# Windowed attention into a rational FFN: the order of the work made by a list scheduler in the source

## The chip, the cores and the metric

The kernel runs on one core of a Trainium2 chip. The metric is the device time of one execution in microseconds (us). The engines are PE (TensorE, matmuls), DVE (VectorE), ACT (ScalarE), POOL (GpSimd) and SP (SyncE, which here only issues DMAs). Each engine works through its own instruction queue in order; an instruction at the head that waits for a semaphore holds everything behind it on the same engine.

## The reference

```python
# q, k, v: (8 batches, 8 heads, 576 positions, 64)
scores = q @ k.T / 8                       # masked to 0 <= i - j < 64
x = softmax(scores) @ v                    # -> x: 4608 tokens x 512
h = x @ w_in                               # w_in 512 x 2048
P = a0 + a1*h + a2*h^2 + a3*h^3
Q = 1 + |b0|*|h| + |b1|*h^2
out = (P / (Q + 1e-6)) @ w_out             # w_out 2048 x 512
```

## The kernel before

The 4608 tokens are nine chunks of 512 (`CH`). A chunk's attention is four units (`unit_load`, `unit_scores`, `unit_transpose`, `unit_av`, one for each pair of heads). A unit loads q, k and v on SP, makes scores on PE (L221), takes the maximum and the exponentials (L228 to L242: eight exponentials on ACT, each followed by the read of its sum), normalises (L246), transposes on PE (L253), copies the result to SBUF on ACT (L255), multiplies with v on PE (L264) and splits the result into a high and a low part, `xh` and `xl` (L269, L270). The band mask is added in one of two ways: for the chunks in `PEM` (here 1 and 2) by two more matmuls on PE (L214), for the others by two DVE passes out of PSUM (L232). Normalising is on DVE for chunk 0 and on POOL for the rest.

The FFN of a chunk is sixteen steps, one for each 128 columns of `w_in`; `steps` lists the 144 of them. `ffn1` makes h with twelve matmuls (L279) and then evaluates the rational function, here called the gate: ACT L286, L287, L288, then DVE L289 and L290 (which read h out of PSUM) beside POOL L291, then ACT L294 and L295, then DVE L296 to L299, which leave the quotient as `gh` and `gl`. `ffn2`, issued `LAG` = 2 steps later, is twelve matmuls (L319) into the chunk's output banks. The gate's temporaries (`ah`, `u`, `num`) have two sets, `gh`/`gl` have three, h has two PSUM banks, which the attention's `ps_x` shares; the scores and the transposed tile share one pair of banks.

The weights arrive as int64 views of pairs and are decoded tile by tile (`decode`): a load on SP, ACT L135, POOL L138, DVE L139 and L140, ACT L143, DVE L144. All 32 decodes must be done once, in the first two chunks; those run as half chunks, `phases` = (0, first half), (1, first half), (1, second half), (0, second half). The second half's weight tiles take the SBUF of the pools `ekv` and `eatt`, which serve chunks 0 and 1 and are closed at step 7 (`SWITCH`).

The order in which things are issued comes from `todo`, a table from step to calls (L341 to L374), and from the loop at L390. That order gives the priorities; the framework's own scheduler (`schedule_with_timeline_sim`, L431) then arranges each engine's queue.

Of the kernel before, what the change touches and what calls it, by code (L numbers as in the profile page):

```python
# [9 lines left out]
F32 = mybir.dt.float32  # L10
# [6 lines left out]
WIN = 64  # L17
# [4 lines left out]
SWITCH = 7  # L22
LAG = 2
W_AT = 0, 1, 2, 3
WLEAD = len(W_AT)
NEG = -1.0e30
PEM = 1, 2
QADD = 1.0 + 1e-6


@with_exitstack
def swa_rational_ffn(ctx: ExitStack, tc: tile.TileContext, qT, kT, v, w_in, w_out, a, b, out):
# [88 lines left out]
    def decode(src, hi, lo):

        w = stage.tile([P, 512, 2], U32, name="w_st", bufs=3)
        if len(src.shape) == 3:
            nc.sync.dma_start(out=w.rearrange("p (c n) two -> p c (n two)", c=src.shape[1]), in_=src)
        else:
            nc.sync.dma_start(out=w.rearrange("p n two -> p (n two)"), in_=src)
        low, high = w[:, :, 0], w[:, :, 1]
        c = stage.tile([P, 512], U32, name="w_c")
        cf = c.bitcast(F32)  # L130

        highf = w.bitcast(F32)[:, :, 1]
        nc.scalar.activation(cf, highf, AF.Copy, scale=2.0 ** -111)  # L135


        nc.gpsimd.tensor_scalar(out=highf, in0=highf, scalar1=0.0, scalar2=None, op0=ALU.mult)  # L138
        nc.vector.scalar_tensor_tensor(out=c, in0=c, scalar=3, in1=high, op0=ALU.logical_shift_left, op1=ALU.bitwise_or)  # L139
        nc.vector.scalar_tensor_tensor(out=c, in0=low, scalar=29, in1=c, op0=ALU.logical_shift_right, op1=ALU.bitwise_or)  # L140
        if len(hi.shape) == 3:
            cf = cf.rearrange("p (c n) -> p c n", c=hi.shape[1])
        nc.scalar.activation(hi, cf, AF.Copy, scale=2.0 ** -8)  # L143
        nc.vector.scalar_tensor_tensor(out=lo, in0=cf, scalar=2.0 ** -8, in1=hi.bitcast(F32), op0=ALU.mult, op1=ALU.subtract)  # L144

    def load_w_in(i):
        decode(w_in[i], wi_h[i], wi_l[i])

    def load_w_out(i):
        decode(w_out_v[:, i, :], wo_h[i], wo_l[i])  # L150
# [12 lines left out]
    def unit_load(c, hp):  # L163
        if c < 2:
            q = ekv.tile([P, TC, WIN], F32, name="q")
            kt = ekv.tile([P, TC + 1, WIN], F32, name="kt")
# [28 lines left out]

    def scores_bank(c, hp):
        if c:
            return ps_a.tile([P, 2, 512], F32, name="ps_s")
        return ps_o.tile([P, 2, DO], F32, name="ps_s", tag=f"o{hp % 2}")

    def unit_scores(c, hp):
        u = live[c, hp]
# [4 lines left out]
        on_pe = c in PEM
        if m0 is None:
            mm = mask[:, 1:2, :].broadcast_to([P, PR, P])
        else:  # L210
# [4 lines left out]
        for p in range(PR):
            for z in range(2):
                for e in range(2):
                    j = 2 * p + e
                    k = u["kt"][z * 64:z * 64 + 64].rearrange("p t s -> p (t s)")
                    w = u["kw"][j] * WIN  # L220
                    nc.tensor.matmul(ps[e * 64:e * 64 + 64, z, p * P:(p + 1) * P], u["q"][z * 64:z * 64 + 64, j, :],  # L221
                                     k[:, w:w + P], start=not on_pe, stop=not on_pe or p == PR - 1)
        sm = pool.tile([P, 2 * PR, P], F32, name="sm")
        NR = 2 * PR
        nmx = pool.tile([P, NR], F32, name="nmx")
        if on_pe:
            pss = ps[:, :, 0:PR * P].rearrange("p z (r c) -> p z r c", c=P)
            nc.vector.tensor_reduce(out=nmx.rearrange("p (z r) -> p z r", z=2), in_=pss, axis=AX.X, op=ALU.max, negate=True)  # L228
            nc.vector.scalar_tensor_tensor(out=nmx, in0=nmx, scalar=SCALE, in1=zero, op0=ALU.mult, op1=ALU.add)
        else:  # L230
            for z in range(2):
                nc.vector.scalar_tensor_tensor(out=sm[:, z * PR:(z + 1) * PR, :],  # L232
                                               in0=ps[:, z, 0:PR * P].rearrange("p (r c) -> p r c", c=P), scalar=SCALE,
                                               in1=mm.bitcast(F32), op0=ALU.mult, op1=ALU.add)
            nc.vector.tensor_reduce(out=nmx, in_=sm, axis=AX.X, op=ALU.max, negate=True)
        sums = pool.tile([P, NR], F32, name="sums")
        for j in range(NR):
            if on_pe:
                nc.scalar.activation(sm[:, j, :], ps[:, j // PR, (j % PR) * P:(j % PR + 1) * P], AF.Exp, scale=SCALE,
                                     bias=nmx[:, j:j + 1], accum_out=sums[:, j:j + 1])  # L240
            else:
                nc.scalar.activation(sm[:, j, :], sm[:, j, :], AF.Exp, bias=nmx[:, j:j + 1], accum_out=sums[:, j:j + 1])  # L242
        rs = pool.tile([P, NR], F32, name="rs")
        nc.vector.scalar_tensor_tensor(out=sums, in0=sums, scalar=1e-9, in1=zero, op0=ALU.add, op1=ALU.add)
        nc.vector.reciprocal(out=rs, in_=sums)
        (nc.vector if c < 1 else nc.gpsimd).tensor_tensor(out=sm, in0=sm, in1=rs.unsqueeze(2).broadcast_to([P, NR, P]), op=ALU.mult)  # L246
        u["sm"] = sm

    def unit_transpose(c, hp):
        u = live[c, hp]  # L250
        ps = ps_a.tile([P, 2, 512], F32, name="ps_s")
        for j in range(2 * PR):
            nc.tensor.transpose(ps[:, j // PR, (j % PR) * P:(j % PR + 1) * P], u["sm"][:, j, :], ident)  # L253
        pT = (eatt if c < 2 else att).tile([P, 2, PR * P], F32, name="pT")
        nc.scalar.copy(out=pT, in_=ps[:, :, 0:PR * P])  # L255
        u["pT"] = pT

    def unit_av(c, hp):
        u = live.pop((c, hp))

        ps = ps_h.tile([P, TC, WIN], F32, name="ps_x", tag="h")
        for j in range(TC):
            for z in range(2):
                nc.tensor.matmul(ps[z * 64:z * 64 + 64, j, :], u["vt"][:, u["vw"][j], z * 64:z * 64 + 64],  # L264
                                 u["pT"][:, z, j * WIN:(j + 1) * WIN], start=True, stop=True)
        xh[c, hp] = xp.tile([P, CH], F32R, name=f"xh{hp}")
        xl[c, hp] = xp.tile([P, CH], F32R, name=f"xl{hp}")
        x = ps.rearrange("p t s -> p (t s)")
        nc.scalar.copy(out=xh[c, hp], in_=x)  # L269
# [38 lines left out]
    def ffn2(s):  # L308
# [11 lines left out]
        if not last:  # L320
            return
# [115 lines left out]
```

## Time and profile before

| | us |
|---|---|
| three runs | 1121.77, 1122.4, 1123.28; median 1122.4 |
| profiled execution | 1124.48, its span 1122.7 |
| PE busy in the span | 991.2 |
| DVE, ACT, POOL busy | 797.6, 675.1, 325.8 |
| first FFN matmul | 46.67 |
| FFN matmuls of step 8, 24, 32, 128 begin | 130.3, 249.0, 321.7, 1021.4 |

The last two rows come from the L279 matmuls in order of time, twelve to a step. Between 321.7 and 1021.4 lie six whole chunks with the attention of the next ones woven in; after 1021.4 one chunk is left, without attention. Busy time counts an instruction from its start to its modelled end; matmuls overlap, so a busy PE is not a PE at its peak. PEclk is the clock granted to PE, as a share of full speed.

### The profile page before, as it was taken

How to read it: one execution, taken by the hardware profiler on the slowest of the kernel's cores; microseconds unless marked ns; L12 is line 12 of the kernel's file. 1: busy time of each engine (PE TensorE's matmuls, PEld its weight loads, DVE VectorE, ACT ScalarE, POOL GpSimd, SP SyncE). 2: the span in 40 equal slices, each digit the busy share in tenths (PEclk: the TensorE clock that was granted, in tenths of full speed). 3: DMA queues.
4: the chain of work that ended last, by engine and by line, in shares of the span. 5: the costliest groups of instructions: out<-in, count | busy, mean ns of one | idle time of the engine just before them, and what ended most of it. 6: DMA issues, size and time to landing. Idle time of an engine off the chain costs nothing.

```text
span 1122.7 us, 16288 instructions
## 1 busy us (share of the span) xinstructions
PE 991.2 (88%) x6064; PEld 765.3 (68%) x6064; DVE 797.6 (71%) x1180; ACT 675.1 (60%) x1471; POOL 325.8 (29%) x223
## 2 busy tenths in 40 slices
PE   4657998698888999999989998999899998989997
PEld 3545776576666777677767776777677766778886
DVE  6886779876755777666667676667766666668775
ACT  4765666557654666655656556655665555666654
POOL 3452335532222222222222222222222222222221
PEclk9767999999999999999999999999999999999999
DMA  9621042322213000310031002110121012001001
GB/s 302 228 89 36 1 129 83 106 70 99 61 50 106 18 21 21 107 37 21 20 107 38 20 20 91 39 41 22 57 81 39 20 40 67 1 1 39 1 1 38
DMA packets 38959, 66.47 MB, mean 59 GB/s; under 512 B 5600, under 2 KB 21984, under 8 KB 38880
## 3 DMA queue, kind: packets, MB, share of 16 engines
q1 hardware_dynamic: 38880, 65.43, 18.4%
q8 instruction: 48, 0.79, 0.3%
q14 instruction: 31, 0.25, 0.1%
HBM read 54.92 MB, written 10.49 MB: 58 GB/s over the span
## 4 chain that ended last, share of the span: by engine, by line
PE 31%; ACT 19%; DVE 14%; POOL 12%; issue 10%; DMA 2%; SPq 0%; POOLq 0%; DVEq 0%; ACTq 0%
PE h L279 16%; PE o L319 11%; POOL u L291 7%; ACT sm L242 5%; POOL sm L246 4%; DVE num L298 3%; ACT ah L294 3%; ACT ah L295 3%; PE ps_x L264 3%; DVE num L289 3%; ACT num L287 2%; DVE gh L296 2%; ACT pT L255 2%; DVE u L297 2%; ACT ah L286 2%
## 5 line engine op out<-in xcount | busy, mean ns | idle before, releaser
L291 POOL TENSOR_TENSOR u<-u,ah 128x512 f32<-128x512 f32 x144 | 197.3, 1371 | 541.5 <-DVE num L289 303.6
L319 PE MATMUL o<-wo_h,gl 128*128 128x512 f32 x576 | 240.9, 418 | 50.1 <-DVE gl L299 46.2
L279 PE MATMUL h<-xl,wi_h 128*128 128x512 f32 x576 | 236.6, 411 | 1.4 <-DVE num L290 1.4
L319 PE MATMUL o<-wo_l,gh 128*128 128x512 f32 x576 | 231.9, 403 | 0.0
L319 PE MATMUL o<-wo_h,gh 128*128 128x512 f32 x576 | 231.7, 402 | 0.0
L279 PE MATMUL h<-xh,wi_l 128*128 128x512 f32 x576 | 227.1, 394 | 0.0
L279 PE MATMUL h<-xh,wi_h 128*128 128x512 f32 x576 | 227.1, 394 | 0.0
L296 DVE SCALAR_TENSOR_TENSOR gh<-num,a_sb,ah 128x512 fp32r<-128x512 f32 x144 | 110.1, 765 | 149.1 <-ACT ah L295 148.8
L294 ACT ACTIVATE ah<-u 128x512 f32<-128x512 f32 x144 | 91.0, 632 | 188.6 <-POOL u L291 188.6
L319 PEld LDWEIGHTS o<-wo_h,gl 128*128 128x128 f32 x576 | 111.2, 193 | 101.1 <-DVE gl L299 61.8
L289 DVE TENSOR_TENSOR num<-num,h 128x512 f32<-128x512 f32 x144 | 98.4, 683 | 96.2 <-ACT num L287 96.0
L286 ACT ACTIVATE ah<-h 128x512 f32<-128x512 f32 x144 | 85.5, 593 | 130.7 <-PE h L279 101.3
L279 PEld LDWEIGHTS h<-xl,wi_h 128*128 128x128 f32 x576 | 108.7, 189 | 35.1 <-issue 9.3
L319 PEld LDWEIGHTS o<-wo_h,gh 128*128 128x128 f32 x576 | 111.7, 194 | 26.2
L319 PEld LDWEIGHTS o<-wo_l,gh 128*128 128x128 f32 x576 | 111.8, 194 | 22.2
L279 PEld LDWEIGHTS h<-xh,wi_l 128*128 128x128 f32 x576 | 108.6, 189 | 25.3
L298 DVE SCALAR_TENSOR_TENSOR num<-num,a_sb,u 128x512 f32<-128x512 f32 x144 | 124.0, 861 | 1.7
L279 PEld LDWEIGHTS h<-xh,wi_h 128*128 128x128 f32 x576 | 109.0, 189 | 21.8
L288 ACT ACTIVATE u<-ah,b_sb 128x512 f32<-128x512 f32 x144 | 117.3, 814 | 0.0
L246 POOL TENSOR_TENSOR sm<-sm,rs 128x1024 f32<-128x1024 f32 x32 | 65.2, 2036 | 176.2 <-ACT num L287 83.5
L287 ACT ACTIVATE num<-h,a_sb 128x512 f32<-128x512 f32 x144 | 111.5, 774 | 0.0
L290 DVE SCALAR_TENSOR_TENSOR num<-num,a_sb,h 128x512 f32<-128x512 f32 x144 | 107.1, 744 | 3.1
(51 smaller groups left out, 1119.6 us busy)
## 6 DMA issues: line engine op xcount, KB each, us to landing
out<-ob SPq DMA_DIRECT2D x36, 256.0 KB, 2.0
w_st<-w_in SPq DMA_DIRECT2D x16, 512.0 KB, 4.7
w_st<-w_out SPq DMA_DIRECT2D x16, 512.0 KB, 3.6
vt<-v SPq DMA_DIRECT2D x8, 448.0 KB, 4.9
vt<-v SPq DMA_DIRECT2D x8, 384.0 KB, 4.1
vt<-v SPq DMA_DIRECT2D x8, 320.0 KB, 3.1
q<-qT SPq DMA_DIRECT2D x8, 256.0 KB, 3.3
kt<-kT SPq DMA_DIRECT2D x8, 256.0 KB, 3.6
```

The lines of the kernel that those rows point to most:

```text
L246: (nc.vector if c < 1 else nc.gpsimd).tensor_tensor(out=sm, in0=sm, in1=rs.unsqueeze(2).broadcast_to([P, NR, P]), op=ALU.mult)
L279: nc.tensor.matmul(h, w[i][:, cc, :], x[c, cc], start=n == 0, stop=n == 3 * NCC - 1)
L286: nc.scalar.activation(ah, h, AF.Abs)
L287: nc.scalar.activation(num, h, AF.Identity, scale=a_sb[:, 3:4], bias=a_sb[:, 2:3])
L288: nc.scalar.activation(u, ah, AF.Identity, scale=b_sb[:, 1:2], bias=b_sb[:, 0:1])
L289: nc.vector.tensor_tensor(out=num, in0=num, in1=h, op=ALU.mult)
L290: nc.vector.scalar_tensor_tensor(out=num, in0=num, scalar=a_sb[:, 1:2], in1=h, op0=ALU.add, op1=ALU.mult)
L291: nc.gpsimd.tensor_tensor(out=u, in0=u, in1=ah, op=ALU.mult)
L294: nc.scalar.activation(ah, u, AF.Ln, bias=QADD)
L296: nc.vector.scalar_tensor_tensor(out=gh, in0=num, scalar=a_sb[:, 0:1], in1=ah, op0=ALU.add, op1=ALU.mult)
L298: nc.vector.scalar_tensor_tensor(out=num, in0=num, scalar=a_sb[:, 0:1], in1=u, op0=ALU.add, op1=ALU.subtract)
L319: nc.tensor.matmul(acc[c][t], g[:, ts], w[i], start=first and n == 0, stop=last and n == 2)
```

## The change

Every piece of work becomes an `Op` with an engine, a cost, a rank (its place in steps), the ops it waits for and the buffer slots it uses. `Plan.order()` is a list scheduler in Python: it walks a clock, starts on each engine the ready op that can start earliest (ties within 0.02 us go to the lower rank), models slots, the DMA bus, PE's slower start after idling, an interface that POOL and some DVE ops share, and the turn-around on PE between kinds of matmuls. The ops are then emitted sorted by their modelled start inside `tc.manual_schedule()`, so the queue of each engine is in that order, and the framework's scheduler no longer arranges them.

With it change:

- `LAG` 2 to 3; `gh`/`gl` keep three sets.
- `phases`: (0, first half), (1, first half), (1, second half), (0, second half) as before.
- `PEM` 1, 2 to 0, 1: chunk 0's mask is added by PE, chunk 2's by DVE.
- Chunk 0's normalising goes from DVE to POOL.
- The early pools become `e0` (chunk 0's q, k, v, four sets, on the left of SBUF) and `e1` (chunk 1's q, k, v and the early softmax tiles, two sets, on the right). `e0` gives way to weight tiles 8 to 11 once chunk 0's products with v are done, `e1` to tiles 12 to 15 once chunk 1's are too.
- `xh`/`xl` have a fixed place for each chunk (`slot_of`).
- The loads of a and b stand ahead of everything else on SP.

The core of the diff:

```diff
-SWITCH = 7
-LAG = 2
-W_AT = 0, 1, 2, 3
-WLEAD = len(W_AT)
+LAG = 3
-PEM = 1, 2
+PEM = 0, 1
+class Plan:
+    LATENCY = 0.035
+    TAIL = {"PE": -0.16, "DVE": 0.083, "ACT": 0.105, "POOL": 0.0, "SP": 0.0}
+    TURN = {("F", "V"): 0.092, ("F", "S"): 0.088, ("V", "S"): 0.122, ("S", "F"): 0.172, ("V", "F"): 0.128,
+            ("T", "V"): 0.05, ("T", "S"): 0.05, ("V", "T"): 0.122, ("S", "T"): 0.1}
...
+    def order(self):
...
+        while len(done) < len(self.ops):
+            best = None
+            for e in ENGINES:
+                able = []
+                for op in ready[e]:
+                    if e == "SP" and op.rank > now + self.ahead:
+                        continue
+                    if any(not slots[s.pool] for s in op.takes):
+                        continue
+                    t = max([free[e], op.ready + op.late] + [min(slots[s.pool]) for s in op.takes])
+                    if op.port:
+                        t = max(t, port["POOL" if e == "DVE" else "DVE"])
...
+                t0 = min(t for t, _ in able)
+                t, op = min(((t, op) for t, op in able if t <= t0 + 0.02), key=lambda x: (x[1].rank, x[0], x[1].n))
+                if best is None or t < best[0]:
+                    best = t, op
...
+        return sorted(self.ops, key=lambda o: o.start)
...
-    gp = ctx.enter_context(tc.tile_pool(name="gp", bufs=LAG + 1))
-    early = ExitStack()
-    ekv = early.enter_context(tc.tile_pool(name="ekv", bufs=4))
-    eatt = early.enter_context(tc.tile_pool(name="eatt", bufs=2))
+    gp = ctx.enter_context(tc.tile_pool(name="gp", bufs=3))
+    e0 = Early(tc, "e0", 4, "left")
+    e1 = Early(tc, "e1", 2, "right")
+    eatt = e1.pool
...
+    plan = Plan({"w_st": 3, "w_c": 2, "kt": 1, "e0": 4, "e1": 2, "sme": 2, "pTe": 2, "sm": 1, "pT": 1, "ps_s": 1, "h": 2,
+                 "tmp": 2, "gp": 3, "o0": 1, "o1": 1}, 4.0)
...
+    late = [Stage(0, e0, range(H, H + H // 2), "left"), Stage(1, e1, range(H + H // 2, NF), "right")]
...
+        o = plan.add("SP", 1.6, rank - 2, load, uses=[st])
+        o = plan.add("ACT", 0.66, rank, scale, [o], [st, sc])
+        o = plan.add("POOL", 1.57, rank, sign, [o], [st], 0.55)
+        o = plan.add("DVE", 0.688, rank, put_sign, [o], [st, sc], 0.688)
+        o = plan.add("DVE", 0.688, rank, put_low, [o], [st, sc], 0.688)
+        o = plan.add("ACT", 0.63, rank, high, [o] + [x for l in late if i in l.tiles for x in held[l.n]], [sc])
+        return plan.add("DVE", 0.688, rank, rest, [o], [sc], 0.688)
...
-        (nc.vector if c < 1 else nc.gpsimd).tensor_tensor(out=sm, in0=sm, in1=rs.unsqueeze(2).broadcast_to([P, NR, P]), op=ALU.mult)
+            nc.gpsimd.tensor_tensor(out=sm, in0=sm, in1=u["rs"].unsqueeze(2).broadcast_to([P, NR, P]), op=ALU.mult)
...
+        o = plan.add("DVE", 1.39 if on_pe else 1.21, r(3), maxima, [o], [ssm, sps] if on_pe else [ssm])
+        o = plan.add("ACT", 3.1, r(4), exps, [o], [ssm, sps] if on_pe else [ssm])
+        o = plan.add("DVE", 0.4, r(5), invert, [o])
+        o = plan.add("POOL", 1.95, r(6), normalise, [o], [ssm], 1.95)
+        o = link("transposes", plan.add("PE", 0.872, r(7), transposes, [o, chain.get("transposes")], [ssm, spt], kind="T"))
+        o = plan.add("ACT", 1.0, r(8), copy_pT, [o], [spt, spT])
+        o = plan.add("PE", 0.97, r(9), values, [o, lv, chain.get("values")] + free_x.get(c, []), [svt, spT, spx], kind="V")
...
+        f = f1[s] = plan.add("PE", 2.76, s, products, x_ready[c] + [tile_in[i], f1.get(s - 1)], [sh])
+        a0 = plan.add("ACT", 0.594, r(1), absolute, [f], [sh, st])
+        n0 = plan.add("ACT", 0.772, r(2), num0, [a0], [sh, st])
+        u_0 = plan.add("ACT", 0.80, r(3), u0, [a0], [st])
+        n1 = plan.add("DVE", 0.688, r(4), num1, [n0], [sh, st])
+        n2 = plan.add("DVE", 0.748, r(5), num2, [n1], [sh, st])
+        u_1 = plan.add("POOL", 1.30, r(5), u1, [u_0], [st], 1.30)
+        o = plan.add("ACT", 0.63, r(6), logarithm, [u_1], [st])
+        o = plan.add("ACT", 0.63, r(7), inverse, [o], [st])
+        g = plan.add("DVE", 0.748, r(8), g_high, [o, n2], [st, sg], 0.748, kind="R")
...
+            o = plan.add("PE", 0.69, s + LAG + 0.5 + 0.01 * t, lambda t=t: products(t),
+                         [gate_done[s], tile_out[i], f2.get((s - 1, t)), f2.get((s, t - 1))], [sg, so[t]])
...
+            tile_in[i] = plan_decode(i, w_in[i], wi_h, wi_l, need[i] - 1.5)
+            tile_out[i] = plan_decode(i, w_out_v[:, i, :], wo_h, wo_l, need[i] + LAG - 1.5)
...
+                order.append((c, k, -12 + k if c == 0 else before + (prev // NU) * k - AHEAD))
...
+    load_coefficients()
+    with tc.manual_schedule():
+        for op in plan.order():
+            op.emit()
```

More of the change, by code (lines that the diff above doesn't have):

```diff
@@ L21, with __init__ @@
 AHEAD = 3
-SWITCH = 7
-LAG = 2
-W_AT = 0, 1, 2, 3
-WLEAD = len(W_AT)
+LAG = 3
 NEG = -1.0e30
-PEM = 1, 2
+PEM = 0, 1
 QADD = 1.0 + 1e-6
+class Slot:
+    def __init__(self, pool):
+        self.pool, self.uses = pool, []
+class Op:
+    def __init__(self, engine, cost, rank, emit, after, uses, port, late, kind):
+        self.engine, self.cost, self.rank, self.emit, self.after = engine, cost, rank, emit, after
+        self.port, self.late, self.kind = port, late, kind
+        self.start = self.end = None
+        uses = list(dict.fromkeys(uses))
+        self.takes = [s for s in uses if not s.uses]
+        for s in uses:
+            s.uses.append(self)
@@ L119, in swa_rational_ffn @@
     w_out_v = w_out.rearrange("(fc p) e -> p fc e", p=P)
[L121 to L150, printed above, removed]
+    C0 = 2
+    HA = 8
+    NU = HP
+    phases = [(c, 0, HA) for c in range(C0)] + [(c, HA, NF) for c in reversed(range(C0))] + [(c, 0, NF) for c in range(C0, NCH)]
+    steps = [(c, i) for c, i0, i1 in phases for i in range(i0, i1)]
+    total = len(steps)
+    begin, at = {}, {}
+    for s, (c, i) in enumerate(steps):
+        begin.setdefault(c, s)
+        at[c, i] = s
@@ L249, in unit_transpose @@
[L249 to L269, printed above, removed]
-        nc.vector.tensor_tensor(out=xl[c, hp], in0=x, in1=xh[c, hp].bitcast(F32), op=ALU.subtract)
@@ L311, in ffn2 @@
         last = s == total - 1 or steps[s + 1][0] != c
+        d, sg = gs.pop(s)
         if first:
-            pair = [ps_o.tile([P, 2, DO], F32, name=f"o{t}") for t in range(NTS // 2)]
-            acc[c] = [pair[t // 2][:, t % 2, :] for t in range(NTS)]
-        gh, gl = gs.pop((c, i))
-        for t in range(NTS):
-            ts = slice(t * P, (t + 1) * P)
-            for n, (g, w) in enumerate(((gl, wo_h), (gh, wo_l), (gh, wo_h))):
-                nc.tensor.matmul(acc[c][t], g[:, ts], w[i], start=first and n == 0, stop=last and n == 2)
@@ L390, in swa_rational_ffn @@
-    for s in range(total + LAG):
-        if s == SWITCH:
-            early.close()
-            weights(ctx.enter_context(tc.tile_pool(name="late", bufs=1, reuse_waits="tile")), range(H, NF))
-        for fn, *args in todo.get(s, ()):
-            if fn in (load_w_in, load_w_out):
-                fn(*args)
-        if s < total:
-            ffn1(*steps[s])
-        for fn, *args in todo.get(s, ()):
-            if fn not in (load_w_in, load_w_out):
-                fn(*args)
-        if s >= LAG:
-            ffn2(s - LAG)
+            for t in range(0, NTS, 2):
+                so[t] = so[t + 1] = Slot(f"o{t // 2}")
@@ new lines, in plan_out, with products @@
+        spill = c < C0 - 1 and i < HA
+        merge = c < C0 - 1 and i >= HA
+        def products(t):
+            if first and t % 2 == 0:
+                pair = ps_o.tile([P, 2, DO], F32, name=f"o{t // 2}")
+                acc[t], acc[t + 1] = pair[:, 0, :], pair[:, 1, :]
+            ts = slice(t * P, (t + 1) * P)
+            for n, (g, w) in enumerate(((d["gl"], wo_h), (d["gh"], wo_l), (d["gh"], wo_h))):
+                nc.tensor.matmul(acc[t], g[:, ts], w[i], start=first and n == 0, stop=last and n == 2)
@@ new lines, in swa_rational_ffn @@
+    last_step = {}
+    for s, (c, i) in enumerate(steps):
+        last_step[c] = s
+    holder = {}
+    n = 0
+    s = 0
+    for c, k, rank in order:
+        if c == C0 and k == 0:
+            plan_tiles()
+        if c >= C0 and k == 0:
+            old = max(x for x in range(c) if slot_of[x] == slot_of[c])
+            while s <= last_step[old]:
+                plan_gate(s)
+                s += 1
+            free_x[c] = [f1[last_step[old]]]
+        plan_unit(c, k, rank)
+    while s < total:
+        plan_gate(s)
+        s += 1
@@ L406 @@
+    for s in range(total):
+        plan_out(s)
+    load_coefficients()
+    with tc.manual_schedule():
+        for op in plan.order():
+            op.emit()
 _OUTS = [((4608, 512), 'float32')]
```

522 lines of the change are left out of this document (354 added, 168 removed).

## The prediction, made before the changed kernel ran

> **What bounds the kernel now.** I read the page first, then the table of busy time by stretch, then the waits inside the long middle stretch, and last the order of time. From the page:
>
> ```profile
> span 1122.7 us, 16288 instructions
> PE 991.2 (88%) x6064; PEld 765.3 (68%) x6064; DVE 797.6 (71%) x1180; ACT 675.1 (60%) x1471; POOL 325.8 (29%) x223
> ...
> PEclk9767999999999999999999999999999999999999
> ```
>
> PE leads, but 131.5 us of the span have no matmul, and the clock granted to PE falls only in the first slices. The stretches below are cut where the FFN matmuls of step 0, 8, 24, 32 and 128 begin; columns are length, then busy time (instructions) of PE, weight load, DVE, ACT and POOL, then granted clock, DMA share, GB/s.
>
> ```profile
> 0.00:46.67 46.67, 23.52 (x304) 19.72 (x304) 34.50 (x52) 28.17 (x89) 16.82 (x23) 0.85 0.80 264
> 46.67:130.26 83.59, 59.83 (x441) 45.89 (x439) 61.72 (x95) 53.05 (x131) 36.69 (x23) 0.82 0.22 73
> 130.26:249.00 118.74, 103.10 (x503) 80.94 (x501) 101.43 (x147) 72.55 (x131) 53.09 (x30) 0.96 0.28 88
> 249.00:321.70 72.70, 63.10 (x475) 49.58 (x472) 45.02 (x71) 45.32 (x117) 18.33 (x13) 0.98 0.23 72
> 321.70:1021.40 699.70, 647.20 (x3942) 492.82 (x3941) 483.39 (x716) 419.79 (x914) 180.12 (x120) 0.99 0.14 43
> 1021.40:1122.70 101.30, 94.41 (x409) 76.38 (x407) 71.52 (x104) 56.26 (x90) 20.76 (x17) 0.99 0.06 21
> ```
>
> The two kinds of stretch differ. Up to 249, where the weights are decoded, PE has no matmul in 62.6 us of 249 and DVE is the fullest engine (198 us). From 321.7 to 1021.4 six whole chunks pass, 116.6 us each, and PE is the fullest. There the waits are (who waits, for whom: total us, times, longest):
>
> ```profile
> POOL u L291 <- DVE num L289: 231.9, 27, 13.7
> ...
> ACT ah L294 <- POOL u L291: 160.8, 93, 3.6
> ...
> PE ps_x L264 <- ACT pT L255: 27.3, 22, 1.3
> ...
> PE o L319 <- DVE gl L299: 22.8, 27, 3.1
> ```
>
> PE's own two waits, 27.3 and 22.8 us, are nearly all of its 52.5 idle us. The first is one hole per attention unit: the transposes, ACT's copy and the products with v stand right behind one another.
>
> ```profile
> 608.86 1.03 PE L253 MATMUL ps_s<-ident,sm 128*128 128x128 f32 x8
> ...
> 610.12 0.99 ACT L255 COPY pT<-ps_s 128x1024 f32<-128x1024 f32 x1
> ...
> 611.16 1.03 PE L264 MATMUL ps_x<-pT,vt 128*64 128x64 f32 x28 [1.27 <-ACT pT L255]
> ```
>
> **The middle stretch, part by part.** What PE must do there is priced from pieces that ran without a hole: 24 FFN matmuls in a row (the chain in order of time), and the three attention pieces with the start of what follows each.
>
> ```profile
> 133.25 5.61 PE o L319 x24
> ```
>
> ```profile
> 75.01 1.06 PE L253 MATMUL ps_s<-ident,sm 128*128 128x128 f32 x8 [0.86 <-issue]
> 75.83 0.48 PE L319 MATMUL o<-wo_h,gl 128*128 128x512 f32 x1
> ...
> 78.82 1.15 PE L264 MATMUL ps_x<-pT,vt 128*64 128x64 f32 x32
> 79.90 1.09 PE L253 MATMUL ps_s<-ident,sm 128*128 128x128 f32 x8
> ...
> 83.84 1.10 PE L221 MATMUL ps_s<-kt,q 64*64 64x128 f32 x32
> 84.87 0.50 PE L279 MATMUL h<-xl,wi_h 128*128 128x512 f32 x1
> ```
>
> A step is 5.61 us. A unit is 0.82 + 1.08 + 1.03 = 2.93, which I round up to 3.2 for three changes of kind. A chunk is 16 × 5.61 + 4 × 3.2 = 102.6, six are 615. So the old order loses 84 us here. The new order treats each piece as one item: the scores are not split, and another FFN piece can stand between transposes and products with v, since the scheduler knows that the copy takes 1.0. If that cover fails (no FFN piece ready), the 27.3 us stay. LAG 3 puts one more step, 5.61 us, between a gate and its second product, which covers the 3.1 of the longest wait for gl. With both gone, what is late next is the gate itself: it has two sets of temporaries, so a third gate waits for the first one's gl.
>
> The other bound is DVE with POOL. If the two never overlapped, a chunk would take (483.39 + 180.12) / 6 = 110.6. The order cannot be counted on to reach either end, as the 231.9 us row puts the end of POOL's waits down to a DVE instruction. I take the middle, 106.6, 640 us for six chunks; both ends are kept, 615 and 664.
>
> ```profile
> L291 POOL TENSOR_TENSOR u<-u,ah 128x512 f32<-128x512 f32 x144 | 197.3, 1371 | 541.5 <-DVE num L289 303.6 <-ACT u L288 237.9
> L298 DVE SCALAR_TENSOR_TENSOR num<-num,a_sb,u 128x512 f32<-128x512 f32 x144 | 124.0, 861 | 1.7
> L296 DVE SCALAR_TENSOR_TENSOR gh<-num,a_sb,ah 128x512 fp32r<-128x512 f32 x144 | 110.1, 765 | 149.1 <-ACT ah L295 148.8
> L299 DVE TENSOR_TENSOR gl<-num,ah 128x512 fp32r<-128x512 f32 x144 | 103.1, 716 | 1.6
> L297 DVE SCALAR_TENSOR_TENSOR u<-u,gh 128x512 f32<-128x512 f32 x144 | 99.8, 693 | 10.9 <-DVE gh L296 0.5
> ...
> L242 ACT ACTIVATE sm<-sm,nmx 128x128 f32<-128x128 f32 x224 | 86.5, 391 | 0.4 <-DVE nmx L235 0.4
> ...
> L246 POOL TENSOR_TENSOR sm<-sm,rs 128x1024 f32<-128x1024 f32 x32 | 65.2, 2036 | 176.2 <-ACT num L287 83.5 <-DVE rs L245 52.4 <-ACT ah L286 33.9
> ...
> L255 ACT COPY pT<-ps_s 128x1024 f32<-128x1024 f32 x36 | 36.0, 1001 | 11.7 <-PE ps_s L253 11.6
> L232 DVE SCALAR_TENSOR_TENSOR sm<-ps_s,mask 128x512 f32<-128x512 f32 x56 | 35.9, 680 | 4.0 <-PE ps_s L221 4.0
> L235 DVE TENSOR_REDUCE nmx<-sm 128x8 f32<-128x1024 f32 x28 | 33.9, 1210 | 0.0
> ...
> L270 DVE TENSOR_TENSOR xl<-ps_x,xh 128x512 fp32r<-128x512 f32 x36 | 24.7, 685 | 16.4 <-ACT xh L269 16.4
> ...
> L269 ACT CAST xh<-ps_x 128x512 fp32r<-128x512 f32 x36 | 21.0, 587 | 44.9 <-PE ps_x L264 31.0 <-PE h L279 13.9
> ...
> L246 DVE TENSOR_TENSOR sm<-sm,rs 128x1024 f32<-128x1024 f32 x4 | 4.9, 1221 | 0.1
> ```
>
> The Trainium skill, GPSIMD Engine Reference, section Key points, says that GpSimd's SBUF interfaces collide only with VectorE instructions that have two SBUF inputs or run in a two-port mode. By it only L296 to L299 and POOL exclude one another: 16 × (0.861 + 0.765 + 0.716 + 0.693 + 1.371) + 4 × 2.036 = 78.6 a chunk, under PE's 102.6, so the lower end would hold. The 861 ns mean of L298, against 765 for L296 with the same kinds of operands, looks like such a collision.
>
> **The first two chunks.** Up to step 24 DVE is the measure: 34.50 + 61.72 + 101.43 = 197.7 us of work. The change takes from it chunk 0's two mask passes, 4 × 2 × 0.68 = 5.4, and its normalising, 4.9; that becomes 4 × 2.04 on POOL. PE gets eight more mask matmuls in chunk 0 and loses eight in chunk 2, where DVE gets the 5.4 back, beside a PE-bound stretch. That leaves 187.4 us. DVE's best long share so far is 101.43 of 118.74, 85%; at that the work takes 220.5. Before it stands the time until DVE's first work on data:
>
> ```profile
> 6.41 1.29 DVE L232 SCALAR_TENSOR_TENSOR sm<-ps_s,mask 128x512 f32<-128x512 f32 x2 [0.90 <-PE ps_s L221]
> ```
>
> I keep 6.4, though the two small loads of a and b now go ahead on SP and the mask must be done before the scores. Steps 24 to 32 are then PE's: 8 × 5.61 + 4 × 3.2 = 57.7. Step 32 begins at 6.4 + 220.5 + 57.7 = 284.6, against 321.7. The bounds: a DVE share of 95% gives 261; no gain gives 321.7.
>
> Why should the share not fall? SP holds its queue in order: a tile's load that waits for one of three staging buffers holds the next unit's q, k and v, and PE waits for those. The early give-away of `e0` after chunk 0 alone lets tiles 8 to 11 be decoded sooner; against that stand two sets, not four, for chunk 1's loads. I cost both at nothing, covered by PE's 62.6 idle us; without that cover a late unit costs PE its 3.2.
>
> **The sum.** After 1021.4 nothing but the FFN is left. PE already runs there; one more step of lag lets the product of step 142 go before the last gate ends, which I put at 2 us: 99.3. Together 284.6 + 640 + 99.3 = 1023.9 of span. The profiled execution took 1124.48 around a span of 1122.7, the median of the runs is 1122.4, so span and median agree within 0.3 us: 1023.
>
> **The rivals.**
>
> *PE's floor* (chance 0.12): 261 + 615 + 98 = 974 to 1000. For it: the skill's rule above, and the last chunk, where PE is busy 94 of 101 us. Against it: units make gates uneven, and the order is fixed for modelled durations.
>
> *DVE and POOL in series* (0.18): 284.6 + 664 + 99.3 = 1048, up to 1066 where the early stretch gains half. For it the 231.9 us row, against it the overlap in the last chunk, 71.5 + 20.8 busy with PE at its peak.
>
> *A cold PE in the first eight steps* (0.05): the clock granted there is 0.82. If DVE-bound gaps hold it at half, eight steps and four units take 8 × 11.2 + 4 × 6.4 = 115 in place of 61.72 / 0.85 = 73: 1066. The Trainium skill, TensorE: Matmul & The Clock Gate, section The HAM clock gate, says that about 3.4 us of idling halve the clock and about 3.4 us of work restore it; the 0.82 agrees with gaps of that size.
>
> *Only the early stretch gains* (0.05): 284.6 + 699.7 + 101.3 = 1086. *The written order gives the same queues* (0.02): 1122.
>
> *Slower: a unit goes through the gates in series* (0.08). The scheduler emits the eight exponentials as one block. In the static queue of ACT the Ln and Exp of both gates in flight wait behind it, DVE's gh behind those, and with two sets of temporaries no third gate starts. Without attention two gates pass in 11.2 us:
>
> ```profile
> 1046.73 0.60 ACT L286 ACTIVATE ah<-h 128x512 f32<-128x512 f32 x1 [3.75 <-PE h L279]
> ...
> 1057.96 0.60 ACT L286 ACTIVATE ah<-h 128x512 f32<-128x512 f32 x1 [3.75 <-PE h L279]
> ```
>
> A unit's chain is 2 × 0.68 + 1.21 + 86.5 / 28 + 2.04 + 1.00 + 0.59 + 0.69 = 9.98. Wholly in series, four steps take 22.4 + 9.98 = 32.4, six chunks 777, the kernel 1161. It is slower than before once more than 8.4 of the 9.98 stay uncovered, (1122.4 − 284.6 − 99.3) / 24 − 22.4; today 116.6 / 4 − 22.4 = 6.7 do. Against it: the 6.7 include PE's holes, which the change fills.
>
> **How the numbers follow.** The forecast's own case, 1000 to 1045, has 0.5. A range from 980 to 1086 leaves out most of the slower case, half of the early-only one, the unchanged one and a little of the floor, not quite two in ten. A measurement of this kernel tells 0.2% from no change. Faster gets all but the slower and the unchanged case: 0.90, 0.02, 0.08.
>
> **What would show it.** Step 32 near 285 with DVE at 85% or more up to step 24; about 107 us a chunk after that; the wait of L264's successor for the copy gone from PE's waits and no split scores; the wait for gl under 5 us. The prediction is wrong if PE's busy share between step 32 and step 128 stays near 92%, if gates wait for exponentials and PE then for h, or if the early stretch shows DVE under 80%.

## The result, and the profile after

The changed kernel takes 1008.05 us, the median of 1007.73, 1008.04, 1008.06 and 1013.41, against 1122.84 (1121.77 to 1124.54) for the kernel before on the same chip: a ratio of 0.8988 with a 95% interval of 0.8956 to 0.902. The profiled execution took 1008.06 around a span of 1006.1, 116.6 us less than the span before. Of the kernel without the sign pass, further down, two of four executions are left out (1548.08 us at a granted PE clock of 0.557, and 2517.24 us at one of 1.0), and what slowed them is open.

The page of the kernel after: span, busy time by engine, granted clock in forty slices, and the chain of waits by engine.

```profile
span 1006.1 us, 16269 instructions
...
PE 951.4 (95%) x6064; PEld 756.4 (75%) x6064; DVE 799.3 (79%) x1176; ACT 670.7 (67%) x1471; POOL 338.9 (34%) x227
...
PEclk9989999988999999999999999999999999999999
...
PE 79%; DVE 12%; ACT 3%; issue 2%; POOL 1%; DMA 1%; SPq 0%; DVEq 0%; POOLq 0%; ACTq 0%
```

The work of each engine is nearly what it was (DVE 799.3 against 797.6), and there is less time around it. The chain that ends last is 79% PE; the same row of the kernel before shares it out:

```profile
PE 31%; ACT 19%; DVE 14%; POOL 12%; issue 10%; DMA 2%; SPq 0%; POOLq 0%; DVEq 0%; ACTq 0%
```

The stretches of the kernel after, cut where the FFN matmuls of step 0, 8, 24, 32 and 128 begin (columns as in the prediction):

```profile
0.00:36.80 36.80, 22.39 (x330) 17.36 (x330) 17.55 (x31) 22.69 (x81) 15.52 (x22) 0.91 0.64 224
36.80:110.70 73.90, 59.56 (x423) 43.77 (x420) 65.14 (x94) 51.45 (x130) 39.08 (x23) 0.91 0.35 112
110.70:221.40 110.70, 95.72 (x418) 74.03 (x417) 104.62 (x146) 70.18 (x115) 50.00 (x32) 0.97 0.30 93
221.40:288.30 66.90, 60.74 (x481) 48.94 (x480) 51.92 (x81) 49.44 (x124) 24.06 (x15) 0.95 0.29 90
288.30:903.40 615.10, 615.09 (x4001) 493.57 (x4000) 484.13 (x726) 419.74 (x932) 181.81 (x121) 1.00 0.16 51
903.40:1006.10 102.70, 97.89 (x421) 78.73 (x419) 75.94 (x103) 57.17 (x90) 28.42 (x17) 1.00 0.06 21
```

Step 32 begins 33.4 us earlier than before, the six chunks after it take 84.6 us less (699.7 to 615.1), and the last chunk takes 1.4 more. In the six chunks PE is busy for 615.09 of 615.10 us and no wait of PE is left. Its weight loads stay at 493 us (492.82 before), which is 80% of the stretch against 70%. The Trainium skill, Perfetto Trace Analysis, section Identifying the Most-Contended Engine, says that matmul busy time is no good measure of how close a kernel is to its bound, as matmuls are pipelined, and names the busy share of the weight loads as one of two measures to use instead. The trace agrees: PE's busy share rose from 92% to 100%, that of the weight loads, for the same work, from 70% to 80%.

The waits of the other engines in that stretch (engine and line, what they waited for; total, times, longest, in us):

```profile
POOL u L547 <- ACT u L537: 214.5, 60, 7.1
ACT ah L550 <- POOL u L547: 90.5, 64, 1.9
POOL u L547 <- DVE num L540: 67.4, 11, 8.5
...
DVE gh L557 <- ACT ah L553: 42.9, 26, 4.0
```

POOL's wait for `num` was 231.9 and ACT's wait for POOL 160.8. They have shrunk, and where they remain they cost nothing, because PE waits for none of them. How one unit now passes PE (start, duration):

```profile
567.79 0.40 PE L525 MATMUL h<-xh,wi_l 128*128 128x512 f32 x1
568.02 1.03 PE L462 MATMUL ps_s<-ident,sm 128*128 128x128 f32 x8
568.81 0.47 PE L609 MATMUL o<-wo_h,gl 128*128 128x512 f32 x1
...
570.05 0.40 PE L609 MATMUL o<-wo_h,gh 128*128 128x512 f32 x1
570.38 1.15 PE L472 MATMUL ps_x<-pT,vt 128*64 128x64 f32 x32
571.46 0.50 PE L609 MATMUL o<-wo_h,gl 128*128 128x512 f32 x1
```

Six matmuls of the FFN stand between the transposes and the products with v, so ACT's copy of the transposed tile is covered.

### The profile page after: what moved, and what is told of

Read it like the earlier page. It is cut to its first block, busy times and chain, and to the rows that moved or that the text cites. A ratio compares the mean times of both kernels' runs of the same rounds, so it can differ in the third digit from the quotient of the medians.

```text
span 1006.1 us, 16269 instructions
## 1 busy us (share of the span) xinstructions
PE 951.4 (95%) x6064; PEld 756.4 (75%) x6064; DVE 799.3 (79%) x1176; ACT 670.7 (67%) x1471; POOL 338.9 (34%) x227
## 4 chain that ended last, share of the span: by engine, by line
PE 79%; DVE 12%; ACT 3%; issue 2%; POOL 1%; DMA 1%; SPq 0%; DVEq 0%; POOLq 0%; ACTq 0%
PE o L609 35%; PE h L525 34%; PE ps_x L472 4%; PE ps_s L419 3%; PE ps_s L462 3%; DVE u L561 2%; DVE w_c L309 1%; DVE gh L557 1%; DVE num L565 1%; DVE w_c L304 1%; DVE num L540 1%; DVE gl L570 1%; DVE num L543 1%; ACT pT L466 1%; POOL sm L457 1%
## 5 line engine op out<-in xcount | busy, mean ns | idle before, releaser
L547 POOL TENSOR_TENSOR u<-u,ah 128x512 f32<-128x512 f32 x144 | 209.6, 1456 | 432.9 <-ACT u L537 264.6
L609 PE MATMUL o<-wo_h,gl 128*128 128x512 f32 x576 | 237.0, 412 | 11.6 <-ACT wo_h L320 6.5
L525 PE MATMUL h<-xl,wi_h 128*128 128x512 f32 x576 | 229.4, 398 | 6.9 <-DVE num L543 5.4
L609 PE MATMUL o<-wo_l,gh 128*128 128x512 f32 x576 | 229.1, 398 | 2.7 <-DVE wo_l L323 2.7
L540 DVE TENSOR_TENSOR num<-num,h 128x512 f32<-128x512 f32 x144 | 98.5, 684 | 51.2 <-ACT num L534 49.7
L457 POOL TENSOR_TENSOR sm<-sm,rs 128x1024 f32<-128x1024 f32 x36 | 70.9, 1970 | 174.7 <-DVE rs L453 78.6
L609 PEld LDWEIGHTS o<-wo_h,gh 128*128 128x128 f32 x576 | 109.3, 190 | 25.5
L565 DVE SCALAR_TENSOR_TENSOR num<-num,a_sb,u 128x512 f32<-128x512 f32 x144 | 114.5, 796 | 1.7
L561 DVE SCALAR_TENSOR_TENSOR u<-u,gh 128x512 f32<-128x512 f32 x144 | 106.4, 739 | 8.5
L570 DVE TENSOR_TENSOR gl<-num,ah 128x512 fp32r<-128x512 f32 x144 | 111.3, 773 | 1.8
```

The lines of the kernel that those rows point to most:

```text
L457: nc.gpsimd.tensor_tensor(out=sm, in0=sm, in1=u["rs"].unsqueeze(2).broadcast_to([P, NR, P]), op=ALU.mult)
L525: nc.tensor.matmul(h, w[i][:, cc, :], x[c, cc], start=n == 0, stop=n == 3 * NCC - 1)
L540: nc.vector.tensor_tensor(out=d["num"], in0=d["num"], in1=d["h"], op=ALU.mult)
L547: nc.gpsimd.tensor_tensor(out=d["u"], in0=d["u"], in1=d["ah"], op=ALU.mult)
L561: nc.vector.scalar_tensor_tensor(out=d["u"], in0=d["u"], scalar=QADD, in1=d["gh"].bitcast(F32), op0=ALU.add, op1=ALU.mult)
L565: nc.vector.scalar_tensor_tensor(out=d["num"], in0=d["num"], scalar=a_sb[:, 0:1], in1=d["u"], op0=ALU.add, op1=ALU.subtract)
```

## Where the 84.6 us of the middle stretch were

The waits of the kernel before add up to 52.5 idle us of PE, and 84.6 were won. The rest, 32.1, stood in PE's busy time, which fell from 647.20 to 615.09 for nearly the same matmuls. To find it, the starts of consecutive matmuls are compared. An FFN matmul of the undisturbed run starts 0.232 us after the one before it (5.57 us for 24).

The kernel before, PE around one wait for `gl`:

```profile
572.01 0.40 PE L319 MATMUL o<-wo_h,gh 128*128 128x512 f32 x1
574.22 0.50 PE L319 MATMUL o<-wo_h,gl 128*128 128x512 f32 x1 [1.81 <-DVE gl L299]
574.55 0.44 PE L319 MATMUL o<-wo_l,gh 128*128 128x512 f32 x1
574.79 0.63 PE L319 MATMUL o<-wo_h,gh 128*128 128x512 f32 x1
575.22 0.63 PE L319 MATMUL o<-wo_h,gl 128*128 128x512 f32 x1
```

The wait is marked 1.81, but from start to start it cost 574.22 − 572.01 − 0.23 = 1.98. Behind it the matmuls start 0.43 apart for the next 3.4 us, and the granted clock there is 0.53:

```profile
575.00:578.40 3.40, 3.40 (x9) 2.65 (x9) 1.44 (x2) 1.93 (x4) 2.58 (x2) 0.53 0.65 224
```

Summed over the stretch in this way for each kernel (waits: starts between two FFN matmuls with a marked wait, less 0.232 each; holes: from the start of the last transpose to that of the first product with v, where nothing stands between them; pieces: how many pieces the scores of the 23 units whose scores lie there come in; all times in us):

```
kernel                               stretch   waits   holes   pieces
before                                 699.7    28.4    33.3      66
before, v one step later               655.9     0.5    35.0      46
before, v one step later, LAG 3        630.4       0       0      46
after, framework arranges              624.0       0       0      44
after, unit held together              643.1       0    33.5      23
after, LAG 2                           618.9     0.5       0      23
after, no shared interface             624.5     3.3       0      23
after                                  615.1       0       0      23
```

So of 84.6 us, 28.4 were the waits. The holes come to 33.3, but some of that is spent without a hole too: the run below that holds the units together again has 33.5 by the same measure, and its stretch is 28.0 longer. About 5 were the half clock behind such waits: some 26 starts about 0.43 apart, 0.2 too long each. The remaining 23 or so fall in the main to the attention's pieces: the scores came in 66 pieces, now in 23. A piece starts about 0.32 after the FFN matmul ahead of it, and the second FFN matmul behind a piece about 0.34 after the first, and not 0.232. Counted from start to start, the scores with what these turns take over 0.232 come to some 47 us in the kernel before and 28 after, about 19 less.

## The experiments

**The framework's scheduler back.** The ops are issued in the planned order, but without the fixed queues.

```diff
-    with tc.manual_schedule():
-        for op in plan.order():
-            op.emit()
+    for op in plan.order():
+        op.emit()
```

> Edit: the same ops are emitted in the same order, but the framework's scheduler may arrange each engine's queue. Theory (the fixed queues are what fills PE): the holes come back in the middle, 1050 to 1110. Rival (the order of emission, the lag and the buffers are enough): 1005 to 1020.

Measured: 1034.74 us, 0.9204 (0.9188 to 0.922). Neither fits. Two windows of it, up to step 0 and steps 32 to 128:

```profile
0.00:54.41 54.41, 25.01 (x331) 19.02 (x331) 29.22 (x45) 28.28 (x91) 24.98 (x27) 0.78 0.60 203
304.47:928.45 623.98, 621.81 (x3993) 493.28 (x3990) 480.91 (x718) 418.27 (x927) 176.71 (x119) 1.00 0.17 51
```

It has no holes and no waits of PE to speak of. The fixed queues are worth about 27 us: 17.6 by step 0 (54.41 against 36.8) and 8.9 in the middle (624.0 against 615.1). Most of the gain, some 89 of 115 us, is in the order of issue and what goes with it, and the framework's scheduler keeps it.

**A unit held together.** For the 28 units of chunks 2 to 8 the transposes and the copy are put back to just before the products with v.

```diff
-        for op in plan.order():
+        ops = plan.order()
+        for tr, cp, va in together[C0 * NU:]:
+            a, b = ops.index(tr), ops.index(va)
...
+            ops = ops[:a] + [o for o in ops[a + 1:b] if o is not cp] + [tr, cp] + ops[b:]
+        for op in ops:
```

> Edit: for chunks 2 to 8 the transposes and the copy are held back to just ahead of the products with v, so that PE waits for the copy again in each of 28 units. Theory (PE is full from step 32 on and nothing else has a claim on the end): 28 x 1.2 to 1.4 = 34 to 39 us more, 1042 to 1047. Rival (DVE with POOL or the two sets of gate temporaries would bound the middle anyway): under 10 us more, up to 1018.

Measured: 1043.06 us, 0.9278 (0.9264 to 0.9292), 35 us above the kernel after. The window from step 32 to 128, and all that PE waited for there:

```profile
293.76:936.90 643.14, 616.14 (x4002) 496.40 (x4001) 483.81 (x726) 423.13 (x932) 180.88 (x121) 1.00 0.16 49
```

```profile
PE ps_x L473 <- ACT pT L467: 27.0, 24, 1.4
```

The stretch is 28.0 longer (step 32 comes 5.5 later too), and the one wait of the kernel before is back at its old size. The holes are shown to be a cost of about 1.2 to 1.4 us a unit.

**Two steps of lag.**

```diff
-LAG = 3
+LAG = 2
```

> Edit: LAG 2 in the planner, nothing else. Theory (the third step of lag covers the waits for gl, 22.8 us of PE's in the middle before): 10 to 25 us more, 1018 to 1033. Rival (the planner finds other work for PE with either lag): within 4 us of 1008.

Measured: 1013.94 us, 0.9017 (0.9002 to 0.9032), which lies between the two; the middle is 618.9, 3.8 more. In the new order the third step of lag is worth about 6 us, and it is not what removed the 28.4 of waits.

**A planner that knows nothing of the interface which POOL and DVE share.**

```diff
-        self.port, self.late, self.kind = port, late, kind
+        self.port, self.late, self.kind = 0.0, late, kind
```

> Edit: the planner no longer knows of the interface that POOL and some DVE ops share. Theory of the prediction (DVE with POOL lies near enough to PE to matter): 8 to 50 us more, the upper end being DVE and POOL in series. Rival (the skill's rule by itself: 78.6 us a chunk of excluding work under 102.6 of PE, so the order need not know): less than 4 us more.

Measured: 1014.43 us, 0.9024 (0.9005 to 0.9042), 6.4 us more, which lies between the two. Its middle:

```profile
283.59:908.06 624.47, 616.35 (x3996) 491.16 (x3995) 497.27 (x726) 421.29 (x930) 185.81 (x120) 1.00 0.16 51
```

DVE's busy time there rises by 13 us and the stretch by 9.4, while step 32 comes 4.7 us earlier. The model of the interface is worth a few us; an order made in ignorance of it is still within 2% of PE's floor in the middle.

**The kernel before with one line moved.** The products with v are issued a step later.

```diff
-                at(p + 1, unit_av, c, k)
+                at(p + 2, unit_av, c, k)
```

> Edit of the kernel before: the products with v are issued one step later than the transposes, nothing else. Theory (PE's hole behind each copy is filled as soon as the source puts other work there): up to 27 us less in the middle, 1095 to 1105. Rival (another wait takes its place in that order): less than 8 us, above 1114.

Measured: 1065.87 us, 0.9483 (0.945 to 0.9517): 58 us from one line, far more than either theory gave, and not in the place expected. PE's two waits from step 32 to 128:

```profile
PE ps_x L264 <- ACT pT L255: 28.7, 23, 2.2
PE o L319 <- DVE gl L299: 0.4, 1, 0.4
```

The holes are all still there; the waits for `gl` are gone. Why shows in DVE's queue. The kernel before, around a wait of PE for the `gl` that starts at 605.19:

```profile
602.30 0.74 DVE L296 SCALAR_TENSOR_TENSOR gh<-num,a_sb,ah 128x512 fp32r<-128x512 f32 x1
603.15 0.69 DVE L297 SCALAR_TENSOR_TENSOR u<-u,gh 128x512 f32<-128x512 f32 x1
604.33 0.17 DVE L244 SCALAR_TENSOR_TENSOR sums<-sums,zero 128x8 f32<-128x8 f32 x1 [0.48 <-ACT sm L242]
604.41 0.74 DVE L298 SCALAR_TENSOR_TENSOR num<-num,a_sb,u 128x512 f32<-128x512 f32 x1
605.07 0.20 DVE L245 RECIPROCAL rs<-sums 128x8 f32<-128x8 f32 x1
605.19 0.69 DVE L299 TENSOR_TENSOR gl<-num,ah 128x512 fp32r<-128x512 f32 x1
```

The kernel with the line moved, DVE:

```profile
572.83 0.74 DVE L296 SCALAR_TENSOR_TENSOR gh<-num,a_sb,ah 128x512 fp32r<-128x512 f32 x1
573.68 0.69 DVE L297 SCALAR_TENSOR_TENSOR u<-u,gh 128x512 f32<-128x512 f32 x1
574.41 0.75 DVE L298 SCALAR_TENSOR_TENSOR num<-num,a_sb,u 128x512 f32<-128x512 f32 x1
575.20 0.69 DVE L299 TENSOR_TENSOR gl<-num,ah 128x512 fp32r<-128x512 f32 x1
576.18 0.17 DVE L244 SCALAR_TENSOR_TENSOR sums<-sums,zero 128x8 f32<-128x8 f32 x1 [0.29 <-ACT sm L242]
```

In the kernel before, the unit's `sums` stands in the middle of a gate and waits there for the last exponential, with the gate's last two instructions behind it. In the middle stretch that is so for 22 of 95 gates, and 19 of PE's 27 waits for `gl` are for these. With the line moved it is so for none of 97, and one wait is left. So by number most of PE's waits for `gl` have `sums` ahead of it in DVE's queue. By time it is less. What `sums` holds up is about 0.5 us of waiting and 0.1 to 0.2 of work: that is all of a short wait, but 0.6 of each of the four of 1.81 and 0.1 of the longest, 3.15, where it did not wait at all. Together that is about 11 of the 28.4 us. What else the moved line changed to remove the rest, and how the framework's scheduler comes to that order from it, stays open, and `sums` was not moved by itself.

**The same with a third step of lag and a fourth set of `gh`/`gl`.**

```diff
-LAG = 2
+LAG = 3
...
-                at(p + 1, unit_av, c, k)
+                at(p + 2, unit_av, c, k)
```

> Edit of the kernel before: as b_split, and LAG 3 with a fourth set of gh and gl. Theory (hole and wait for gl are the two losses of the middle): 40 to 50 us less than before, 1072 to 1084. Rival (the finer order of the planner, in which even a single output bank's products are an item of their own, is what counts): above 1090.

Measured: 1044.12 us, 0.9286 (0.9266 to 0.9306), below the expected range; its middle is 630.4, and FFN matmuls now stand in every hole. Two small edits of the old source give 80 of the 115 us. What stays is 15.3 us in the middle, where PE still waits 16 times for the copy behind those matmuls (9.2 us, the longest 0.6) and the scores come in 46 pieces against 23, and 21.8 before step 32.

**Early give-away of `e0` undone.** Both groups of late weight tiles wait for chunk 0 and chunk 1.

```diff
-            if c == 0:
-                held[1].append(o)
+            held[1 - c].append(o)
```

> Edit of the changed kernel: both groups of late weight tiles wait for chunk 0 and chunk 1, as with the one give-away of before. Theory (the late tiles are not due before step 14, when chunk 1 is long done): within 3 us of 1008. Rival (the first give-away is what lets DVE start on the late tiles): 8 us or more.

Measured: 1008.19 us, 0.8976 (0.8959 to 0.8993). Nothing, as priced.

**DVE's share of the early stretch.** One of the three DVE passes of each decode is left out: first the sign, then, in another kernel, the low bits.

```diff
-        o = plan.add("DVE", 0.688, rank, put_sign, [o], [st, sc], 0.688)
```

> Edit of the changed kernel: each weight decode leaves out the DVE pass that puts in the sign (L304), so the weights are wrong; everything else is planned anew. Theory (DVE bounds the stretch up to step 24): 32 x 0.69 = 22 us of DVE work less, 18 to 24 us less, 984 to 990. Rival (loads, ACT or a cold PE bound it): less than 8 us, above 1000.

Measured: 987.26 and 989.92 us, 0.8797 (0.8772 to 0.8822), some 20 us less. The other pass:

```diff
-        o = plan.add("DVE", 0.688, rank, put_low, [o], [st, sc], 0.688)
```

> Edit of the changed kernel: each weight decode leaves out the DVE pass that puts in the three lowest bits (L309), so the weights keep their size and are off in their last bits; everything else is planned anew. Theory (DVE bounds the stretch up to step 24): 32 x 0.69 = 22 us of DVE work less, 18 to 24 us less, 984 to 990, all of it before step 32. Rival (loads, ACT or a cold PE bound it): less than 8 us, above 1000.

Measured: 990.58 us, 0.8819 (0.8792 to 0.8846). Up to step 24, and steps 24 to 32:

```profile
0.00:204.16 204.16, 174.17 (x1165) 135.96 (x1166) 159.60 (x237) 143.78 (x328) 104.04 (x77) 0.93 0.41 132
204.16:270.92 66.76, 61.93 (x494) 48.16 (x492) 55.04 (x83) 49.35 (x124) 22.89 (x14) 1.00 0.27 82
```

32 × 0.69 = 22 us of DVE's work are gone, and step 32 comes 17.4 us earlier, nearly all of it by step 24 (17.2). Nothing changes after that. DVE's passes in the decodes are shown to set the early stretch, at 80% of each us taken from them. Leaving one out also shortens each decode's own chain, and these two runs do not tell that from DVE's time; the next one adds work to DVE outside the decodes.

**Masks of chunk 0 back on DVE, those of chunk 2 on PE.**

```diff
-PEM = 0, 1
+PEM = 1, 2
```

> Edit of the changed kernel: the masks of chunks 1 and 2 by PE and those of chunk 0 by DVE, as before. Theory: 5.4 us of DVE work come into the stretch that DVE bounds, 4 to 6 us more, less what chunk 2 gives back: 1009 to 1014. Rival (DVE is still idle while chunk 0 runs, so its masks cost nothing there, and chunk 2's cost more): 1000 to 1007.

Measured: 1014.33 us, 0.9024 (0.9007 to 0.9041), 6 us more; step 32 begins 6.0 later (294.29), the middle is the same (614.9). Step 24 begins 14.3 later (235.65), and steps 24 to 32 take 58.6 in place of 66.9, with more of chunk 2's attention done ahead of them.

**A version with the early work ranked anew.** Weight tiles of the first eight steps are ranked further ahead, chunk 1's and 2's units later, SP may look further ahead, PE's modelled costs are raised by 1%; masks of chunks 0, 1 and 2 on PE, and in a second kernel those of 0 and 1 only.

```diff
+PEM = 0, 1, 2
...
-                 "tmp": 2, "gp": 3, "o0": 1, "o1": 1}, 4.0)
+                 "tmp": 2, "gp": 3, "o0": 1, "o1": 1}, 5.0)
...
-        f = f1[s] = plan.add("PE", 2.76, s, products, x_ready[c] + [tile_in[i], f1.get(s - 1)], [sh])
+        f = f1[s] = plan.add("PE", 2.79, s, products, x_ready[c] + [tile_in[i], f1.get(s - 1)], [sh])
...
-            o = plan.add("PE", 0.69, s + LAG + 0.5 + 0.01 * t, lambda t=t: products(t),
+            o = plan.add("PE", 0.6975, s + LAG + 0.5 + 0.01 * t, lambda t=t: products(t),
...
-            tile_in[i] = plan_decode(i, w_in[i], wi_h, wi_l, need[i] - 1.5)
-            tile_out[i] = plan_decode(i, w_out_v[:, i, :], wo_h, wo_l, need[i] + LAG - 1.5)
+            tile_in[i] = plan_decode(i, w_in[i], wi_h, wi_l, need[i] - (11 if i < H else 2))
+            tile_out[i] = plan_decode(i, w_out_v[:, i, :], wo_h, wo_l, need[i] + LAG - (3 if i < H else 1))
...
-                order.append((c, k, -12 + k if c == 0 else before + (prev // NU) * k - AHEAD))
+                order.append((c, k, -12 + k if c == 0 else before + (prev // NU) * k - {1: -1, 2: 2}.get(c, AHEAD)))
```

> Edit of the changed kernel: the first eight weight tiles are ranked ahead (11 steps before their need, 3 before for w_out), chunk 1's units four steps later, chunk 2's one later with masks by PE, SP may look 5 steps ahead, and PE's pieces are costed at 0.2325 us a matmul. Theory (DVE has work for 17.55 of the first 36.80 us, and those are lost to a stretch that it bounds): 8 to 15 us less, 993 to 1000. Rival (loads and ACT fill the start, so that earlier decodes only delay chunk 0): within 4 us of 1008 or slower.

> Edit: as the run above, but chunk 2's masks stay on DVE. Theory (after step 24 DVE still has decodes left, so 5.4 us of masks there cost their time): 3 to 6 us slower than the run above. Rival (from step 24 on PE is the bound): the same within 2 us.

Measured: 1003.83 us, 0.8931 (0.8917 to 0.8944), and 1004.29 us, 0.8938 (0.8924 to 0.8951). Both beat the two kernels of the case, by less than expected. Steps 24 to 32 of the first:

```profile
212.96:284.64 71.68, 65.63 (x499) 51.59 (x498) 58.02 (x86) 49.26 (x121) 24.58 (x15) 0.95 0.32 97
```

Step 24 comes 8.4 us earlier, but steps 24 to 32 take 4.8 more; the middle takes 614.8. A third chunk with its masks on PE or on DVE makes no difference, so chunk 2's two passes on DVE are covered.

## Why the prediction was right, and by how much its terms were off

**Way and place: right.** Forecast 1023, measured 1008. Early stretch, middle and end were forecast at 284.6, 640 and 99.3; they came out at 288.3, 615.1 and 102.7. That the first of these is within 4 us is partly luck: step 24 came 5.5 us sooner than forecast, and steps 24 to 32 took 9.2 longer.

**The middle is the term that was mis-sized, by 25 us.** The prediction had the floor, 615, from pieces that ran without a hole, and it was met within 0.1, with some luck: a step takes 5.57 and not 5.61, and what is left of the stretch for its 24 units is 3.36 each and not 3.2, which cancel. What failed is the choice of the middle between the two ends, for the reason that an order with modelled durations could not be counted on to reach either. The run without the interface model shows how little the order depends on that part of the model: 624.5; other durations were not varied by themselves. The 231.9 us row on which the upper end leaned was POOL waiting for DVE, while PE itself waited some 24 us for DVE (22.8 of them for `gl`) and not once for POOL. The rule of the shared interface, by which DVE and POOL exclude each other for 78.6 us a chunk and the floor holds, would have given 998.9 with the other two terms as forecast. Its rival, DVE and POOL in series, is refuted: 110.6 a chunk were forecast, 102.5 taken.

**What was removed: right on the holes, wrong on the cause of the `gl` waits.** Pulling the unit apart covers the copy, as said, and holding it together brings 28.0 us back in the middle. But "LAG 3 ... covers the 3.1 of the longest wait for gl" is not what happened: with LAG 2 the new order loses 3.8, and in the old source one moved line removes the waits with LAG still 2. In 19 of 27 `sums` stood ahead of `gl` in DVE's queue, which accounts for about 11 of the 28.4 us; the cause of the rest is open. The scores in pieces and the slow clock behind waits, some 24 us together, stood under PE's busy time; only the floor, counted from pieces, had them.

**Up to step 24: right, with the share too low.** DVE's work was forecast at 187.4 and is 17.55 + 65.14 + 104.62 = 187.3. Its share from its first work on data to step 24 was forecast at 85%; it is 185.2 of 221.4 − 9.2 = 212.2 us, 87% (2.1 us of casts lie ahead), with the first work on data at 9.2, 2.8 later than the 6.4 that was kept:

```profile
9.19 1.23 DVE L433 TENSOR_REDUCE nmx<-ps_s 128x8 f32<-128x1024 f32 x1 [3.68 <-PE ps_s L419]
```

The two errors give 221.4 for 226.9. Taking a DVE pass from each decode moves step 24 by 17.2, and 5.4 us of masks put back on DVE, outside the decodes, move step 32 by 6.0. That this stretch hangs on DVE's passes is shown; how much of it is DVE's time and how much the length of a decode's chain is not.

**Steps 24 to 32: wrong, 66.9 for 57.7.** They were taken as PE's alone. PE is busy for 60.74 of them, and all that it waits for is this:

```profile
PE ps_s L462 <- POOL sm L457: 3.2, 1, 3.2
PE h L525 <- DVE num L543: 2.9, 1, 2.9
```

The second wait ends at 246.41, when this `num` is done, and a stretch at a granted clock of 0.55 follows. The rows of DVE ahead of it have the last passes of the decodes among those of the gate, and one instruction of 2.38 us:

```profile
242.03 0.64 DVE L309 SCALAR_TENSOR_TENSOR w_c<-w_st,w_c 128x512 uint32<-128x512 uint32 x1
242.59 2.38 DVE L565 SCALAR_TENSOR_TENSOR num<-num,a_sb,u 128x512 f32<-128x512 f32 x1
244.90 0.68 DVE L540 TENSOR_TENSOR num<-num,h 128x512 f32<-128x512 f32 x1
245.61 0.75 DVE L543 SCALAR_TENSOR_TENSOR num<-num,a_sb,h 128x512 f32<-128x512 f32 x1
246.27 0.69 DVE L323 SCALAR_TENSOR_TENSOR wo_l<-w_c,wo_h 128x512 fp32r<-128x512 f32 x1
```

The 3.5 us of PE behind the wait:

```profile
247.50:251.00 3.50, 3.50 (x12) 2.72 (x11) 1.49 (x3) 2.48 (x4) 0.79 (x1) 0.55 0.00 0
```

That the decodes are what makes these steps long is not shown: here the last one ends at 246.96, 25.6 us behind the start of step 24, in the kernel without the low bits 13.3 (217.44), and there the steps take 66.8 all the same. In the version with new ranks what step 24 gains is half lost again in these steps. What would shorten them further stays open.

**The end: 102.7 for 99.3.** The 2 us of the longer lag were there: PE's wait for `gl` behind step 128, 2.0 in the kernel before, is gone. But a third step of lag leaves twelve more matmuls behind the start of step 128 (421 against 409), 12 × 0.232 = 2.8, which the prediction didn't count. That makes 0.8 of the 1.4 by which the end grew; the rest is open. With LAG 2 the new order takes 102.7 as well, with 409 matmuls and 2.4 us of that wait.

**Edits costed at nothing.** The early give-away is worth nothing (1008.19 without it). The masks moved to PE were costed as 5.4 us of DVE's work; moved back they cost 6. That DVE gets those of chunk 2 for nothing holds: 1003.83 and 1004.29. The normalising moved to POOL and the loads of a and b ahead were not run by themselves.

**The other rivals.** The cold PE did not come: the clock granted in the first eight steps is 0.91, above the 0.82 of before. The unit in series through the gates, the slower case, is refuted by the empty list of PE's waits in the middle; DVE's wait for ACT's Exp, `gh` behind `ah`, fell from 114.7 us to 42.9. The queues did change: without the fixed ones the time is 1034.74.

## What to carry to other kernels

When an engine that bounds a stretch looks 92% busy, count its work from the start-to-start times of pieces that ran undisturbed and compare the sum with the stretch: here that gave 615 of 700 us, and so both the loss, busy time included, and the time that a better order reached. Before writing a planner, look at what stands ahead of the late instruction in its own engine's queue and try one line of the issue order; here that gave half of the gain, and with one more step of lag two thirds. And where a chain of waits names one engine for another, ask first if the bounding engine waits for either.

## What the runs showed of the hardware that was not expected

**Half clock after a short wait.** A wait of 1.81 us (574.22, above) was followed by 3.4 us at a granted clock of 0.53. The Trainium skill, TensorE: Matmul & The Clock Gate, section The HAM clock gate, gives about one window of 3.4 us of idling as the condition and says that the window runs freely; the length of the slow piece agrees, the idling here was shorter than the window. The wait of 1.81 comes four times. Behind three of them the matmuls start 0.43 apart, but behind the one that ends at 811.36 the clock stays at 1.00 (811.40 to 814.80). That agrees with a window that runs freely, but no run here varies it. The waits of 0.5 us, and those of 1.2 to 1.5, left the clock at full.

**A DVE instruction that lasts as long as POOL's.** In the DVE rows above, L565 at 242.59 takes 2.38 us where its mean in the middle stretch is 0.777. POOL at that time, in the kernel after:

```profile
242.29 2.13 POOL L457 TENSOR_TENSOR sm<-sm,rs 128x1024 f32<-128x1024 f32 x1 [6.18 <-DVE rs L453]
244.39 1.71 POOL L547 TENSOR_TENSOR u<-u,ah 128x512 f32<-128x512 f32 x1
```

It reads three SBUF tiles, and it ends 0.55 us after POOL's instruction, which ends at 244.42. The next, L540 and L543, read one operand from PSUM and run at their usual 0.68 and 0.75 beside POOL's L547. That agrees, in single instructions, with the rule that the prediction took from the Trainium skill, GPSIMD Engine Reference, section Key points.
